# Attention followed by an MLP: equal key chunks, grouped matmuls, and one more unit of lag between the two

## The chip, the cores and the metric

The kernel runs on one core of a Trainium2 chip. The metric is the time of one execution on the device in microseconds (us). Each run also carries a state: on one core, an execution more than 1.5% above the fastest of the same kernel counts as slow and is left out of comparisons. A ratio in this text is the mean time of one kernel's fast runs over that of the other's fast runs of the same rounds, so it is not quite the ratio of the medians quoted beside it. The "granted clock" is the share of PE's full clock that the trace records.

The engines are PE (matmuls; PEld is its weight load), ACT (exponentials, cosines, copies), DVE (vector work), POOL (more vector work) and SP, which here only issues DMAs. Each works through its own list of instructions in the order in which the program emits them and waits for the others by semaphores.

## The reference

```
# q, k, v: [8, 12, 448, 64] f32; tau = 0.1; w_in: [768, 2048]; w_out: [2048, 768]
q_n = q / (norm(q) + 1e-6);  k_n = k / (norm(k) + 1e-6)
attn = softmax(q_n @ k_n.T / tau)          # 448 x 448 for each of 96 heads
x = (attn @ v) laid out as [3584, 768]     # batch and token, head and dim
h = x @ w_in
out = (h * cos(h)) @ w_out                 # [3584, 768] f32
```

## The kernel before

A "unit" is half a batch: six heads, handled as three "pairs" of two heads. There are 16 units and 48 pairs. Two units make one batch of 448 tokens, whose MLP follows later, between the attention work of later units. A batch's first MLP product, with its cosine and its multiplication into gT, is called an MLP block below (8 groups of 12 matmuls); the second product (112 matmuls of 384 columns per batch on average) is doled out in small "fills".

The 448 keys of a head are cut into three chunks of 128 and a tail of 64. In the tail, the two heads of a pair sit in the two halves of the partitions, so its matmuls use other shapes of the PE array:

```python
    def scores(g, c):                       # transposed scores of one chunk, both heads
        j = g % 2
        z = nq[0] % 2                       # two score buffers, SC0 and SC1
        nq[0] += 1
        for a in range(2):
            r = slice(64 * a, 64 * a + 64)
            if c < NC3:                     # chunk of 128 keys
                PE: matmul(sc[:, a, 0:S], qkT[j][r, 128 keys of chunk c], qkT[j][r, 0:S])
            else:                           # tail: 64 keys, output on half of the partitions
                PE: matmul(sc[r, 0, 0:S], qkT[j][r, S : S + TL], qkT[j][r, 0:S])
        ACT: PX[j, c] = exp(sc / TAU)       # 128 x 896, for the tail 128 x 448

    # av_step(g, c): value matmuls of chunk c for both heads, accumulated in bank 0 of AV
    # av_sums(g):    matmuls with ones, 32 columns wide, for the row sums, in bank 1 of AV;
    #                then ACT copies both banks to xu
```
(The bodies are shortened to what is computed.) The row sums go by DMA from xu to another layout ("gather"), DVE takes the reciprocal ("recip"), two more DMAs spread it through DRAM over the partitions ("spread", "broadcast" into RB), and DVE multiplies ("normalise", into xT, the input of the MLP). The order inside a unit, where kq counts steps of one chunk:

```python
    def unit(u, per_quantum):
        for kq in range(4 * UP):
            p, c = kq // 4, kq % 4
            g = UP * u + p
            scores(g, c)
            if c == 1 and g + 1 < NG:
                transposes(g + 1)           # 7 matmuls, then DVE copies to qkT
            # ... loads, squares, norms, scales of unit u + 1 ...
            if u == 0 and kq >= 2 or u == 1:
                load_w(1)                   # one of 10 weight loads
            # ... recip, spread, broadcast, normalise of earlier units ...
            if per_quantum:
                m2_fill(per_quantum[kq % len(per_quantum)])   # 4, 5 or 6 matmuls into PO
            if g >= 1:
                if c in (1, 2):
                    av_step(g - 1, 2 * c - 2)
                    av_step(g - 1, 2 * c - 1)
                if c == 2:
                    av_sums(g - 1)
                if kq == 3:
                    gather(u - 1)
            if u % 2 == 1 and u >= 3 and kq == M1_AT:
                m1((u - 3) // 2)            # the MLP block of the batch before
```

A fill writes one bank, PO, of PSUM, the memory that takes PE's results. After 16 of its matmuls one output half is complete, DVE copies it to osb, and only then can the next half begin.

Of the kernel before, what the change touches and what calls it, by code (L numbers as in the profile page):

```python
# [140 lines left out]
def bass_cosine_attention__then__act_gcu_kernel(  # L141
# [12 lines left out]
    NP2 = NH // 2  # L154
    NU = 2 * B
    UP = 3
    UH = 2 * UP
    NC3 = 3
    MAIN = NC3 * 128
    TL = S - MAIN  # L160
    NS = 7
# [5 lines left out]
    NT = (B * S) // 128  # L167
# [21 lines left out]
    xT = sbs("xT", 2, [128, NP2 * S], BF16)  # L189
    gT = sb("gT", [128, NF * RING], BF16)  # L190
    raw = sbs("raw", 2, [128, UH * NS * D], F32)
    vraw = sb("vraw", [128, UH * 4 * D], F32)
    sq = sbs("sq", UP, [128, 2 * NS * D], BF16)
    n2 = sbs("n2", 2, [128, UH * NS], F32)
    lnn = sbs("lnn", 2, [128, UH * NS], F32)
    rn = sbs("rn", 2, [128, UH * NS], F32)
    qks = sbs("qks", 2, [128, NS * UH * D], BF16)
    va = sbs("va", 2, [128, UH * 4 * D], BF16)
    qkT = sbs("qkT", 2, [128, NS * 128], BF16)
    PX = sbs("PX", 2, [128, 2 * NC3 * S + S], BF16)  # L200
# [4 lines left out]
    ones = sb("ones", [128, 32], BF16)  # L205
    cosb = sbs("cosb", 2, [128, 2 * S], F32)
    osb = sbs("osb", 3, [128, DM], F32)
    ident = sb("ident", [128, 128], BF16)
    iot = sb("iot", [128, 128], I32)
    cst = sb("cst", [128, 4], F32)  # L210
# [5 lines left out]

    W1v = W1.ap().rearrange("p (c n) -> p c n", c=NKC)
    W2v = W2.ap().rearrange("p (f n) -> p f n", f=NF)
    xTv = [t.ap().rearrange("p (c m) -> p c m", c=NP2) for t in xT]
    gTv = gT.ap().rearrange("p (f m) -> p f m", f=NF)  # L220
    rawv = [t.ap().rearrange("p (h s d) -> p h s d", h=UH, s=NS) for t in raw]
    vrawv = vraw.ap().rearrange("p (h c d) -> p h c d", h=UH, c=4)
    qksv = [t.ap().rearrange("p (s h d) -> p s h d", s=NS, h=UH) for t in qks]
    vav = [t.ap().rearrange("p (x c) -> p x c", c=D) for t in va]
    PXm = [t.ap()[:, 0 : 2 * NC3 * S].rearrange("p (c a s) -> p c a s", c=NC3, a=2) for t in PX]
    PXt = [t.ap()[:, 2 * NC3 * S :] for t in PX]
# [5 lines left out]
    PHs = [("SC0", SCv[0]), ("SC1", SCv[1]), ("AV", AVv)]  # L232

    scr = nc.dram_tensor("scr", (NU, UH * S), F32)

    NORM = 11
    M1_AT = 2
# [3 lines left out]
    P.op("POOL", lambda e: e.iota(iot.ap(), [[1, 128]], base=0, channel_multiplier=-1), writes=["iot"])  # L241
# [3 lines left out]
    P.op("POOL", lambda e: e.memset(vrawv[:, :, 3, :], 1.0), writes=["vraw"])  # L245
# [3 lines left out]

    def load(u, p0, p1):  # L250
        i = u % 2
        b, hb = u // 2, UH * (u % 2)
        ha, hn = hb + 2 * p0, 2 * (p1 - p0)
        keys = [("raw", i, p) for p in range(p0, p1)]
        sem = "raw%d_%d" % (i, p0)

        def src(t, tok, n, run):
            return bass.AP(t.tensor, ((b * NH + ha) * S + tok) * D, [[run, n], [S * D, hn], [1, run]])

        h = slice(2 * p0, 2 * p1)  # L260
        P.op("SP", lambda e: e.dma_start(rawv[i][:, h, 0:3, :].rearrange("p h s d -> p h (s d)"),
                                         src(q, 0, 128, NC3 * D)), writes=keys, dma=sem)
        for key_fn in (
            lambda e: e.dma_start(rawv[i][:, h, 4:7, :].rearrange("p h s d -> p h (s d)"),
                                  src(k, 0, 128, NC3 * D)),
            lambda e: e.dma_start(rawv[i][0:TL, h, 3, :], src(q, MAIN, TL, D)),
            lambda e: e.dma_start(rawv[i][64 : 64 + TL, h, 3, :], src(k, MAIN, TL, D)),
        ):
            o = P.op("SP", key_fn, dma=sem)
            for t in keys:  # L270
                P.writer[t] = o

    def load_v(u):
        b, hb = u // 2, UH * (u % 2)

        def src(h0, step, nh, tok, n, run):
            return bass.AP(v.tensor, ((b * NH + hb + h0) * S + tok) * D, [[run, n], [step * S * D, nh], [1, run]])

        P.op("SP", lambda e: e.dma_start(vrawv[:, :, 0:3, :].rearrange("p h c d -> p h (c d)"),
                                         src(0, 1, UH, 0, 128, NC3 * D)), writes=["vraw"], dma="vraw")  # L280
        for a in range(2):
            o = P.op("SP", lambda e, a=a: e.dma_start(vrawv[64 * a : 64 * a + TL, 0::2, 3, :],
                                                      src(a, 2, UP, MAIN, TL, D)), dma="vraw")
            P.writer["vraw"] = o


    def squares(u, p, eng="POOL"):
        i = u % 2
        j = p
        src = raw[i].ap()[:, p * 2 * NS * D : (p + 1) * 2 * NS * D]  # L290
        if eng == "ACT":
            P.op("ACT", lambda e: e.activation(sq[j].ap(), src, ACT.Square), [("raw", i, p)], [("sq", j)])
        else:
            P.op(eng, lambda e: e.tensor_tensor(sq[j].ap(), src, src, ALU.mult), [("raw", i, p)], [("sq", j)])  # L294

    def reduce(u, p):
        i = u % 2
        j = p
        P.op("DVE", lambda e: e.tensor_reduce(out=n2[i].ap()[:, p * 2 * NS : (p + 1) * 2 * NS],  # L299
                                              in_=sq[j].ap().rearrange("p (x d) -> p x d", d=D),  # L300
                                              axis=mybir.AxisListType.X, op=ALU.add),
             [("sq", j)], [("n2", i, p)])

    def rnorm(u, p0, p1):
        i = u % 2
        w = slice(p0 * 2 * NS, p1 * 2 * NS)
        P.op("ACT", lambda e: e.activation(lnn[i].ap()[:, w], n2[i].ap()[:, w], ACT.Ln, bias=cst.ap()[:, 1:2]),
# [4 lines left out]
    def scale(u, p, eng="POOL"):  # L312
        i = u % 2
        h = slice(2 * p, 2 * p + 2)
        P.op(eng, lambda e: e.tensor_tensor(  # L315
            qksv[i][:, :, h, :].rearrange("p s h d -> p h s d"), rawv[i][:, h, :, :],
            bass.AP(rn[i], p * 2 * NS, [[UH * NS, 128], [NS, 2], [1, NS], [0, D]]), ALU.mult),
            [("raw", i, p), ("rn", i, p)], [("qks", i, p)])

    def vcast(u, p):  # L320
        i = u % 2
        P.op("POOL", lambda e: e.tensor_copy(vav[i][:, 8 * p : 8 * p + 8, :],
                                             vrawv[:, 2 * p : 2 * p + 2, :, :].rearrange("p h c d -> p (h c) d")),
             ["vraw"], [("va", i, p)])


    def transposes(g):
        u, p, j = g // UP, g % UP, g % 2
        i = u % 2
        for s in range(NS):  # L330
            P.op("PE", lambda e, s=s: e.transpose(TP.ap()[:, 128 * s : 128 * s + 128],  # L331
                                                  qksv[i][:, s, 2 * p : 2 * p + 2, :], ident.ap()),
                 [("qks", i, p), "ident"], ["TP"])
        P.op("DVE", lambda e: e.tensor_copy(qkT[j].ap(), TP.ap()[:, 0 : NS * 128]), ["TP"], [("qkT", j)])  # L334

    nq = [0]

    def scores(g, c):
        j = g % 2
        z = nq[0] % 2  # L340
        nq[0] += 1
        sc = SCv[z]
        for a in range(2):
            r = slice(64 * a, 64 * a + 64)
            rhs = qkT[j].ap()[r, 0:S]
            if c < NC3:
                P.op("PE", lambda e, r=r, a=a, rhs=rhs: e.matmul(  # L347
                    sc[:, a, 0:S], qkT[j].ap()[r, S + TL + 128 * c : S + TL + 128 * c + 128], rhs,
                    start=True, stop=True), [("qkT", j)], ["SC%d" % z])
            else:  # L350
                P.op("PE", lambda e, r=r, rhs=rhs: e.matmul(  # L351
                    sc[r, 0, 0:S], qkT[j].ap()[r, S : S + TL], rhs, start=True, stop=True),
                    [("qkT", j)], ["SC%d" % z])
        if c < NC3:
            P.op("ACT", lambda e: e.activation(PXm[j][:, c], sc[:, :, 0:S], ACT.Exp, scale=1.0 / TAU),  # L355
                 ["SC%d" % z], [("PX", j, c)])
        else:
            P.op("ACT", lambda e: e.activation(PXt[j], sc[:, 0, 0:S], ACT.Exp, scale=1.0 / TAU),
                 ["SC%d" % z], [("PX", j, c)])

    def av_step(g, c):
        u, p, j = g // UP, g % UP, g % 2
        i = u % 2
        for a in range(2):
            r = slice(64 * a, 64 * a + 64)
            k = slice(0, 128) if c < NC3 else r
            px = PXm[j][:, c, a, :] if c < NC3 else PXt[j][r, :]
            P.op("PE", lambda e, r=r, k=k, a=a, px=px: e.matmul(  # L368
                AVv[r, 0, 0:S], vav[i][k, 8 * p + (4 * a + c if c < NC3 else NC3), :], px, start=(c == 0), stop=(c == NC3)),
                [("va", i, p), ("PX", j, c)], ["AV"])  # L370

    def av_sums(g):
        u, p, j = g // UP, g % UP, g % 2
        i = u % 2
        for c in (0, 1, 2, 3):
            for a in range(2):
                o = slice(64 * a + 32 * (c % 2), 64 * a + 32 * (c % 2) + 32)
                k = slice(0, 128) if c < NC3 else slice(64 * a, 64 * a + 64)
                px = PXm[j][:, c, a, :] if c < NC3 else PXt[j][k, :]
                P.op("PE", lambda e, o=o, k=k, px=px, c=c: e.matmul(  # L380
# [255 lines left out]
```

## Time and profile before

Three runs: 592.94, 594.56 and 594.91 us, median 594.56. A further, profiled run spans 589.0.

The first lines of the page of the kernel before. A busy time is followed by its share of the span and the number of instructions; each digit is the busy share of one fortieth of the span, in tenths:

```profile
span 589.0 us, 7661 instructions
PE 491.1 (83%) x3152; PEld 217.4 (37%) x3152; DVE 234.7 (40%) x300; ACT 290.9 (49%) x358; POOL 192.0 (33%) x159
PE   1380366989998999899898999889898999896997
```

In the first seven fortieths, about 103 us, PE is idle much of the time; after that it is nearly always busy. So there are two regimes: a start-up in which data and its preparation arrive too slowly, and a long stage in which PE sets the pace.

Four of PE's waits in the kernel before (engine, line, tile, who released it: us in total, times, the longest); the left-out ones belong to the start-up or are under 6 us:

```profile
PE SC L347 <- ACT PX L355: 23.6, 3, 21.8
PE PO L477 <- DVE osb L485: 16.0, 22, 2.2
PE SC L351 <- DVE gT L437: 7.1, 3, 2.4
PE AV L432 <- DVE xT L418: 5.2, 1, 5.2
```

The first line is one hole of 21.8 us at 44.7 us. There unit 2's keys come only at 59 us, behind ten weight loads that were all issued during unit 0. The other lines are PE waiting for the copy out of PO, for the last product of an MLP block, and for normalised data.

What PE does inside the long stage is seen in the timeline of one pair before (start, us, line, operation, tile, shape, count). The cost of a group is the distance from its start to the next start, since the shown durations run past the start of the next group:

```profile
120.67 0.38 PE L351 MATMUL SC<-qkT 64*64 64x448 bf16 x2 [2.37 <-DVE gT L437]
120.98 0.82 PE L477 MATMUL PO<-W,gT 128*128 128x384 bf16 x4
121.74 0.36 PE L347 MATMUL SC<-qkT 64*128 64x448 bf16 x2
122.03 0.82 PE L477 MATMUL PO<-W,gT 128*128 128x384 bf16 x4
122.79 0.36 PE L347 MATMUL SC<-qkT 64*128 64x448 bf16 x2
123.08 0.56 PE L331 MATMUL TP<-ident,qks 128*128 128x128 bf16 x7
123.48 0.81 PE L477 MATMUL PO<-W,gT 128*128 128x384 bf16 x4
124.23 0.57 PE L368 MATMUL AV<-PX,va 128*64 128x448 bf16 x4
...
125.78 0.69 PE L368 MATMUL AV<-PX,va 128*64 128x448 bf16 x4
126.39 0.85 PE L380 MATMUL AV<-PX,ones 128*32 128x448 bf16 x8
127.17 0.38 PE L351 MATMUL SC<-qkT 64*64 64x448 bf16 x2
```

The pair takes 127.17 - 120.67 = 6.50 us, although PE never waits inside it. Four PO matmuls take 0.76 us here. In a dense block they take 0.65 (16 of them 2.60). The missing 0.11 us appears wherever the array's shape changes (128\*128 to 64\*128, to 128\*64, to 64\*64), and here the shape changes at nearly every line. (The cut leaves out another score pair and another four PO matmuls.)

### The profile page before, as it was taken

The numbers are of one execution on the slowest core, as the hardware profiler recorded it, in microseconds if no ns is written. First come the engines' busy times: TensorE is split into PE (matmuls) and PEld (weight loads), VectorE is DVE, ScalarE is ACT, GpSimd is POOL, SyncE is SP. The second block draws the span as 40 slices with busy tenths as digits, with TensorE's granted clock in tenths as the row PEclk, the third lists the DMA queues.
The fourth block names the chain that finished last, engine by engine and source line by source line (L and its number), as shares of the span: only waits on it lengthen the run. The fifth ranks groups of instructions, "written<-read, shape, count | busy, mean of one in ns | idle before, by whom it ended". The sixth has DMA issues, their size and how long they took to land.

```text
span 589.0 us, 7661 instructions
## 1 busy us (share of the span) xinstructions
PE 491.1 (83%) x3152; PEld 217.4 (37%) x3152; DVE 234.7 (40%) x300; ACT 290.9 (49%) x358; POOL 192.0 (33%) x159
## 2 busy tenths in 40 slices
PE   1380366989998999899898999889898999896997
PEld 0120122533353444433353444433353344332554
DVE  4300352436444543534345543534354532322421
ACT  3270474466646555556546554555546555550420
POOL 3860854055503480074304380075205240000000
PEclk9996597999999999999999999999999999998999
DMA  6699777015800852045701761145702320122013
GB/s 190 139 225 216 175 191 189 1 50 169 242 3 18 224 143 75 25 115 146 203 2 44 200 170 47 27 123 147 192 1 61 90 76 0 29 77 74 0 55 81
DMA packets 74498, 62.36 MB, mean 106 GB/s; under 512 B 29152, under 2 KB 68064, under 8 KB 74464
## 3 DMA queue, kind: packets, MB, share of 16 engines
q1 hardware_dynamic: 71488, 55.58, 35.4%
q0 software_dynamic: 2976, 6.29, 5.7%
q8 instruction: 25, 0.41, 0.3%
q14 instruction: 9, 0.07, 0.0%
HBM read 56.62 MB, written 11.18 MB: 115 GB/s over the span
## 4 chain that ended last, share of the span: by engine, by line
PE 68%; DMA 15%; DVE 6%; SPq 6%; POOL 2%; ACT 2%; issue 2%; DVEq 0%; ACTq 0%
PE PO L477 20%; PE SC L432 17%; PE AV L432 9%; DMA raw<-in_k_dram 6%; PE AV L368 6%; DMA RB<-scr 5%; PE AV L380 4%; PE SC L347 4%; PE TP L331 3%; PE SC L477 2%; DVE osb L485 2%; DMA sums<-xu 2%; POOL sq L294 2%; PE SC L351 2%; DVE gT L437 1%
## 5 line engine op out<-in xcount | busy, mean ns | idle before, releaser
L355 ACT ACTIVATE PX<-SC 128x896 bf16<-128x896 f32 x144 | 131.2, 918 | 84.8 <-PE SC L347 83.4
L477 PE MATMUL PO<-W,gT 128*128 128x384 bf16 x784 | 155.3, 329 | 19.8 <-DVE osb L485 16.0
L315 POOL TENSOR_TENSOR qks<-raw,rn 128x896 bf16<-128x896 f32 x47 | 79.4, 1689 | 253.5 <-ACT rn L309 253.5
L432 PE MATMUL SC<-xT,W 128*128 128x448 bf16 x516 | 104.4, 359 | 4.2 <-DVE xT L418 4.2
L477 PEld LDWEIGHTS PO<-W,gT 128*128 128x128 bf16 x784 | 65.4, 98 | 76.7 <-DVE osb L485 23.3
L294 POOL TENSOR_TENSOR sq<-raw 128x896 bf16<-128x896 f32 x47 | 80.5, 1739 | 29.3 <-DMA raw<-in_k_dram 29.3
L347 PE MATMUL SC<-qkT 64*128 64x448 bf16 x288 | 53.8, 373 | 34.0 <-ACT PX L355 23.6
L437 DVE TENSOR_TENSOR gT<-SC,cosb 128x896 bf16<-128x896 f32 x43 | 47.0, 1092 | 69.7 <-ACT cosb L435 69.7
L383 ACT ACTIVATE xu<-AV 128x896 f32<-128x896 f32 x48 | 44.0, 917 | 55.9 <-PE AV L380 55.9
L435 ACT ACTIVATE cosb<-SC,cst 128x896 f32<-128x896 f32 x43 | 43.3, 1007 | 56.1 <-PE SC L432 56.1
L432 PEld LDWEIGHTS SC<-xT,W 128*128 128x128 bf16 x516 | 50.9, 99 | 53.8 <-issue 9.2
L299 DVE TENSOR_REDUCE n<-sq 128x14 f32<-128x896 bf16 x48 | 50.7, 1078 | 31.1 <-POOL sq L294 26.9
L368 PE MATMUL AV<-PX,va 128*64 128x448 bf16 (+1 forms) x384 | 61.9, 380 | 0.0
L432 PE MATMUL AV<-xT,W 128*128 128x448 bf16 x252 | 53.4, 364 | 7.2 <-DVE xT L418 5.2
L418 DVE TENSOR_TENSOR xT<-xu,RB 128x448 bf16<-128x448 f32 x48 | 38.2, 808 | 51.3 <-DMA RB<-scr 51.3
L334 DVE COPY qkT<-TP 128x896 bf16<-128x896 bf16 x48 | 29.8, 621 | 65.3 <-PE TP L331 65.3
L485 DVE COPY osb<-PO 128x384 f32<-128x384 f32 x49 | 27.1, 554 | 57.3 <-PE PO L477 57.3
L331 PE MATMUL TP<-ident,qks 128*128 128x128 bf16 x336 | 28.8, 230 | 21.0 <-POOL qks L315 11.0
L347 PEld LDWEIGHTS SC<-qkT 64*128 64x128 bf16 x288 | 13.8, 93 | 81.1 <-issue 36.6
L435 ACT ACTIVATE cosb<-AV,cst 128x896 f32<-128x896 f32 x21 | 21.1, 1007 | 42.7 <-PE AV L432 42.7
L380 PE MATMUL AV<-PX,ones 128*32 128x448 bf16 (+1 forms) x384 | 40.9, 361 | 0.0
L437 DVE TENSOR_TENSOR gT<-AV,cosb 128x896 bf16<-128x896 f32 x21 | 22.9, 1092 | 38.1 <-ACT cosb L435 38.1
(35 smaller groups left out, 246.8 us busy)
## 6 DMA issues: line engine op xcount, KB each, us to landing
RB<-scr SPq DMA_DIRECT2D x32, 336.0 KB, 4.6
vraw<-in_v_dram SPq DMA_DIRECT2D x16, 576.0 KB, 4.6
raw<-in_q_dram SPq DMA_DIRECT2D x15, 576.0 KB, 5.9
raw<-in_k_dram SPq DMA_DIRECT2D x15, 576.0 KB, 6.4
out_dram<-osb SPq DMA_DIRECT2D x32, 192.0 KB, 2.7
out_dram<-osb SPq DMA_DIRECT2D x12, 384.0 KB, 2.9
W<-in_moe_w_in_dram POOLq DMA_DIRECT2D x6, 512.0 KB, 10.7
W<-in_moe_w_out_dram POOLq DMA_DIRECT2D x4, 768.0 KB, 20.1
```

The costliest lines, as they stand in the source:

```text
L294: P.op(eng, lambda e: e.tensor_tensor(sq[j].ap(), src, src, ALU.mult), [("raw", i, p)], [("sq", j)])
L299: P.op("DVE", lambda e: e.tensor_reduce(out=n2[i].ap()[:, p * 2 * NS : (p + 1) * 2 * NS], in_=sq[j].ap().rearrange("p (x d) -> p x d", d=D ...
L315: P.op(eng, lambda e: e.tensor_tensor(qksv[i][:, :, h, :].rearrange("p s h d -> p h s d"), rawv[i][:, h, :, :], bass.AP(rn[i], p * 2 * NS, ...
L331: P.op("PE", lambda e, s=s: e.transpose(TP.ap()[:, 128 * s : 128 * s + 128], qksv[i][:, s, 2 * p : 2 * p + 2, :], ident.ap()), [("qks", i, ...
L347: P.op("PE", lambda e, r=r, a=a, rhs=rhs: e.matmul(sc[:, a, 0:S], qkT[j].ap()[r, S + TL + 128 * c : S + TL + 128 * c + 128], rhs, start=Tr ...
L355: P.op("ACT", lambda e: e.activation(PXm[j][:, c], sc[:, :, 0:S], ACT.Exp, scale=1.0 / TAU), ["SC%d" % z], [("PX", j, c)])
L368: P.op("PE", lambda e, r=r, k=k, a=a, px=px: e.matmul(AVv[r, 0, 0:S], vav[i][k, 8 * p + (4 * a + c if c < NC3 else NC3), :], px, start=(c ...
L380: P.op("PE", lambda e, o=o, k=k, px=px, c=c: e.matmul(AVv[o, 1, 0:S], ones.ap()[k, :], px, start=(c < 2), stop=(c >= 2)), ["ones", ("PX", ...
L432: P.op("PE", lambda e, n=n, c=c, a=a: e.matmul(ph[:, a, 0:S], W1v[:, c, 128 * n : 128 * n + 128], xTv[b % 2][:, c, :], start=(c == 0), sto ...
L435: P.op("ACT", lambda e: e.activation(cosv[cz], ph[:, :, 0:S], ACT.Sin, bias=cst.ap()[:, 0:1], scale=1.0), [name, "cst"], [("cos", cz)])
L437: P.op("DVE", lambda e: e.tensor_tensor(gTv[:, 2 * gidx : 2 * gidx + 2, S * (b % 2) : S * (b % 2) + S], ph[:, :, 0:S], cosv[cz], ALU.mult) ...
L477: P.op("PE", lambda e, po=po, f=f, col=col, hf=hf: e.matmul(po[:, 0:HW], gTv[:, f, col : col + 128], W2v[:, f, HW * hf : HW * hf + HW], st ...
```

## The change

It has five parts:

1. The keys are cut into four chunks of 112 with no tail, so all chunks have one shape and every load is a run of 1 KB. The tail's exponential grows from 448 to 896 columns, and the squares and scales on POOL from 896 to 1024 elements.
2. Two chunks of scores are issued together, and all AV matmuls and sums of a pair in one block.
3. Fills come in blocks of 8 instead of 4 to 6, and 16 stand behind each MLP block, to cover the wait for gT.
4. An MLP block comes one unit later, so that its input has long been normalised. Until the MLP starts, DVE instead of ACT copies AV to xu.
5. Weights come in 20 pieces, six per unit, instead of 10 nearly at once.

The diff cut to its core (cuts marked with "..."):

```diff
-    NC3 = 3
-    MAIN = NC3 * 128
-    TL = S - MAIN
-    NS = 7
+    NJ = 4
+    NP = S // NJ
+    NS = 2 * NJ
...
     def scores(g, c):
-        j = g % 2
-        z = nq[0] % 2
+        j, z = g % 2, c % 2
...
+            P.op("PE", lambda e, r=r, a=a: e.matmul(
+                SCv[z][0:NP, a, 0:S], qkT[j].ap()[r, S + NP * c : S + NP * c + NP], qkT[j].ap()[r, 0:S],
+                start=True, stop=True), [("qkT", j)], ["SC%d" % z])
+        P.op("ACT", ... ACT.Exp ...)          # one form for every chunk
...
+    LAG = 4
+    FILLS = ((8, 8, 8, 8, 8, 8, 8, 8, 8, 0, 8, 0), (8, 8, 8, 8, 16, 8, 8, 8, 8, 8, 8, 16))
...
+    def around(u, kq):                        # all work off PE, by step, as in unit() before
+        ...
+        if kq % 2 == 1:
+            load_w()
+        if u >= 1:
+            if kq == 2:
+                gather(u - 1)
+            if kq == 5:
+                recip(u - 1)
+                spread(u - 1)
+            if kq == 8:
+                broadcast(u - 1)
+        if u >= 2 and kq < UP:
+            normalise(u - 2, kq)
...
     for u in range(NU):
-        b = (u - 3) // 2
-        ...
-        unit(u, fills)
+        for p in range(UP):
+            g = UP * u + p
+            scores(g, 0)
+            scores(g, 1)
+            if g >= 1:
+                attend(g - 1, "DVE" if u < LAG else "ACT")
+            around(u, 4 * p)
+            m2_fill(steps.pop(0) if steps else 0)
+            if g + 1 < NG:
+                transposes(g + 1)
+            around(u, 4 * p + 1)
+            scores(g, 2)
+            scores(g, 3)
+            around(u, 4 * p + 2)
+            m2_fill(steps.pop(0) if steps else 0)
+            around(u, 4 * p + 3)
+            if p == 0 and u >= LAG and u % 2 == 0:
+                m1((u - LAG) // 2)            # 8 groups, then m2_fill(16)
+                steps = list(FILLS[((u - LAG) // 2) % 2])
...
+    # tail: the last but one MLP block, m2_fill(16), m2_fill(80), the last block, m2_fill(16), the rest
```

## The prediction

> **What bounds the kernel now.** The page: PE busy 83% of a 589.0 us span. By windows: to 97.8 us is start-up, PE busy 40 us; then six periods of about 65 us (two units, one MLP block), PE 58 to 62 us busy at full clock; from 525 an MLP tail. Start-up is bound by loads and POOL, the rest by PE. PE's list of waits: 21.8 us at 44.7 (timeline: unit 2's k lands only at 59, behind ten weight loads issued in unit 0; DMA share 1.14 there), 16.0 us on the osb copy of the one PO bank, 7.1 us after MLP blocks on gT, 9.4 us on xT.
>
> **PE costs, start to start in the timeline.** A pair (120.67 to 127.17) takes 6.50 us with 16 second-MLP matmuls. Dense ones take 0.1625 us, so 3.9 us is attention. Every change of array shape costs 0.10 to 0.12 us: 4 second-MLP matmuls 0.76 instead of 0.65, one score pair 0.29 instead of 0.19, four AV 0.50 instead of 0.375. The Trainium skill (TensorEngine Tiling (Array Packing), Key Properties) says that changing the tiling mode drains the TensorE; these starts agree. Four scores in a row took 0.49: the drain is per group.
>
> **The change on PE.** Per pair: two groups of four scores 0.98, AV in one group 0.88, sums as two concurrent fours 0.50 (0.78 before: the tail made extra shapes), transposes 0.41, two second-MLP groups of 8, 2.82. Sum 5.6 us against 6.5. I add 0.3 because the second score buffer's exponential (0.92 us) ends just when the next score step wants it. Period: 6 x 5.9 + first MLP 18.2 + 16 matmuls behind it 2.6 = 56; with 1.5 of stalls 57.5, against 65.4. The 16 matmuls cover the gT wait and the table load; groups of 8 put the osb copy under attention work. Six periods: about -47 us.
>
> **Costs added.** ACT: the tail's exponential goes from 539 to 918 ns, 4.6 us per pair, below PE's 5.9. POOL squares and scales grow by 8/7, to 13.3 us per unit. One more unit passes without MLP; a batch of MLP moves into the tail.
>
> **Start-up.** Weights go out six pieces per unit, so unit 2's k no longer waits. POOL with issues takes about 17 us per unit; about 18.6 MB must land, at up to 240 GB/s (the saturated window). Loads become 1 KB runs (768 and 256 B before); the skill (DMA: Bandwidth & Descriptors, Specifications) wants at least 512 B for line rate; the page counts 29152 packets under that. I expect the first MLP block at 88 to 95 us (97.8 before), one unit further on.
>
> **Tail.** Two first-MLP blocks 36.4, about 240 second-MLP matmuls 39, stalls 4, end 4.3: about 85 us, without the 5.2 us wait on xT.
>
> **Sum.** 92 + 338 + 85 = 515 span; timed runs lie 5.5 above it: 520. With 2 for stalls unseen: 522 us, range 503 to 548. Chances: faster 0.96, within 2% 0.03, slower 0.01.
>
> **Right or wrong.** Distance of MLP blocks in the PE timeline 57 us (wrong if over 61); a plain pair 5.6 to 6.0 us; sums group 0.5 us; no 22 us gap near 45 us; PE waits on osb under 8 us; PE share above 86%.
>
> **What would make it wrong.** POOL or loads keeping start-up at 100 us or more; ACT (exponentials and the AV copy in one queue) ruling the pairs; DVE, in order, held up by RB and delaying qkT; 112-wide matmuls that do not overlap as 128-wide ones do.

## The result, and the profile after

The kernel after takes 541.41 us (median of 4 runs, 538.33 to 543.38), against 594.73 for the kernel before in the same rounds. The ratio is 0.910, with a 95% interval of 0.905 to 0.915. All four runs are fast ones, and the profiled one spans 538.9 us.

The page of the kernel after:

```profile
span 538.9 us, 7716 instructions
PE 471.6 (88%) x3200; PEld 230.7 (43%) x3200; DVE 257.7 (48%) x311; ACT 288.4 (54%) x344; POOL 220.5 (41%) x169
PE   1477674798999999999999999999899999779896
```

The long stage is denser now: almost only nines. The start-up is not shorter. Eight fortieths of this shorter span, 108 us, stay below nine.

One pair of the kernel after, from the timeline. PE waits for nothing in it that the view marks:

```profile
193.14 0.69 PE L314 MATMUL SC<-qkT 64*112 64x448 bf16 x4
193.76 0.95 PE L325 MATMUL AV<-PX,va 112*64 112x448 bf16 x8
194.64 0.56 PE L331 MATMUL AV<-PX,ones 112*32 112x448 bf16 x8
195.13 1.47 PE L420 MATMUL PO<-W,gT 128*128 128x384 bf16 x8
196.44 0.56 PE L305 MATMUL TP<-ident,qks 112*128 112x112 bf16 x8
196.93 0.59 PE L314 MATMUL SC<-qkT 64*112 64x448 bf16 x4
197.45 1.47 PE L420 MATMUL PO<-W,gT 128*128 128x384 bf16 x8
```

Seven groups instead of twelve, the same 16 PO matmuls, and 5.71 us (the next pair starts at 198.85) instead of 6.50. The lines also show that a new group alone costs nothing: the eight PO matmuls at 195.13 take 1.31 us to the transposes, which use the full array as they do (dense ones take 1.30), and those at 197.45 take 1.40 to the scores, whose shape differs.

Three of PE's waits in the kernel after (two left out, of 10.8 and 8.1 us, belong to the start-up, and the other three are 2.4 us or less):

```profile
PE SC L314 <- ACT PX L317: 16.7, 26, 2.4
PE SC L314 <- DVE qkT L308: 13.6, 5, 5.2
PE PO L420 <- DVE osb L428: 9.5, 12, 3.1
```

The hole of 21.8 us is gone, as are the waits on xT. Another has grown: scores waiting for qkT, 13.6 us in five pieces, all before 110 us (3.3 us in the kernel before). Of the first line, 11.8 us fall into the same stretch.

The span can be split at two events in the timeline: the start of the first MLP block, and the start of the first of the two blocks that run after the last attention.

| | predicted | kernel after |
|---|---|---|
| first MLP block starts | 92 us | 110.1 us |
| from there to the first tail block | 338 us | 334.5 us |
| from there to the end | 85 us | 94.3 us |
| span | 515 us | 538.9 us |

In the kernel before, the first MLP block starts at 97.8 us, with one unit less done, and the six periods to the seventh block take 390.4 us. So the periods went from 65.1 to 55.75 us, a gain of 56 us, while the start-up was 18 us and the tail 9 us longer than I had said.

**Where the start-up went.** The timeline of DVE in the kernel after (the bracket gives its idle time and what ended it):

```profile
64.00 2.06 DVE L371 TENSOR_TENSOR xT<-xu,RB 128x448 bf16<-128x448 f32 x1 [1.59 <-DMA RB<-scr]
65.98 0.61 DVE L308 COPY qkT<-TP 128x896 bf16<-128x896 bf16 x1
```

PE had finished the transposes behind that qkT copy at 62.05. The copy started only at 65.98, because the normalising stands before it in DVE's list: it waited 1.59 us for the DMA that fills RB and then took 2.06 us itself (0.61 the next time). PE's next scores waited with it, 3.69 us. PE was slow here besides: eight AV matmuls took 1.71 us at 58.69, against 0.95 in the pair above. The Trainium skill (Perfetto Trace Analysis, Tensor Engine Instruction) calls ACT, DVE and GPSIMD "strict FIFO", and here the trace shows it for DVE.

SP's list in the same stretch shows what these DMAs meet:

```profile
56.57 1.10 SPq L364 DMA_DIRECT2D RB<-scr  x2
58.17 0.32 SPq L259 DMA_DIRECT2D vraw<-in_v_dram  x1
58.53 0.57 SPq L252 DMA_DIRECT2D raw<-in_q_dram  x1
59.15 1.98 SPq L252 DMA_DIRECT2D raw<-in_k_dram  x1
62.44 5.99 SPq L345 DMA_DIRECT2D sums<-xu  x1
```

The DMAs that fill RB were issued before the loads, so no queue held them up; the second landed at 63.98, 6.9 us later, while the loads moved beside it. The gather of the next sums is another matter. It is four DMAs of 5 KB, each normally issued in 0.6 us. Here it comes behind 2 MB of loads for a later unit, and the first takes 6 us to issue. Up to 110 us, sums take 9.2 us (median) from issue to landing, against 3.8 us in the same stretch of the kernel before. The two figures are not quite like for like: in the kernel before, the loads hold SP before the gather is issued (one for 14.04 us, at 28.83), and that time is not in them. In e_schedule below, the median is 3.6 us and the start-up no shorter.

DVE's waits up to 110 us in the kernel after that concern this round trip, and POOL's main wait from 12 to 110 us:

```profile
DVE rcp L353 <- DMA sums<-xu: 14.0, 3, 6.3
DVE xT L371 <- DMA RB<-scr: 6.1, 2, 4.5
POOL qks L290 <- ACT rn L283: 21.9, 4, 9.9
```

POOL, which I had expected to set the pace, waits 22 us for norms. Those come from DVE's sums of squares, which stand in the same list.

**Where the tail went.** The timeline behind the first tail block:

```profile
462.74 1.46 PE L420 MATMUL PO<-W,gT 128*128 128x384 bf16 x8
464.04 1.09 DVE L386 TENSOR_TENSOR gT<-SC,cosb 128x896 bf16<-128x896 f32 x1 [1.18 <-ACT cosb L384]
465.05 1.69 DVE L371 TENSOR_TENSOR xT<-xu,RB 128x448 bf16<-128x448 f32 x3
466.65 0.55 DVE L428 COPY osb<-PO 128x384 f32<-128x384 f32 x1
467.26 4.26 PE L420 MATMUL PO<-W,gT 128*128 128x384 bf16 x16 [3.06 <-DVE osb L428]
```

The same 16 matmuls take 2.77 us elsewhere. After the wait of 3.06 us they took 4.26, on a slower clock (PE's granted clock is 0.93 from 462.7 to 487.4). Five more waits of about 0.7 us follow, one per half, because there is only one PO bank. The tail also held 264 second-MLP matmuls instead of my 240. Two entries of the fill list, 8 and 16, are never used before the loop ends.

### The profile page after: what moved, and what is told of

Same layout as the page of the kernel before. It is cut to its first block, busy times and chain, and to the rows that moved or that the text cites. A ratio compares the mean times of both kernels' runs of the same rounds, so it can differ in the third digit from the quotient of the medians.

```text
span 538.9 us, 7716 instructions
## 1 busy us (share of the span) xinstructions
PE 471.6 (88%) x3200; PEld 230.7 (43%) x3200; DVE 257.7 (48%) x311; ACT 288.4 (54%) x344; POOL 220.5 (41%) x169
## 2 busy tenths in 40 slices
DMA packets 51490, 62.36 MB, mean 116 GB/s; under 512 B 9984, under 2 KB 44288, under 8 KB 51456
## 4 chain that ended last, share of the span: by engine, by line
PE 64%; DMA 16%; DVE 10%; ACT 4%; SPq 3%; POOL 2%; issue 1%; DVEq 0%; ACTq 0%
PE PO L420 20%; PE SC L381 16%; PE AV L381 10%; DMA sums<-xu 6%; DMA RB<-scr 6%; PE AV L325 5%; PE SC L314 5%; PE AV L331 3%; DMA raw<-in_k_dram 3%; DVE xT L371 3%; ACT PX L317 3%; PE SC L420 2%; DVE n L273 2%; PE TP L305 2%; SPq L345 2%; DMA scr<-rcp 2%
## 5 line engine op out<-in xcount | busy, mean ns | idle before, releaser
L317 ACT ACTIVATE PX<-SC 112x896 bf16<-112x896 f32 x192 | 164.0, 915 | 85.8 <-PE SC L314 85.8
L290 POOL TENSOR_TENSOR qks<-raw,rn 112x1024 bf16<-112x1024 f32 (+1 forms) x48 | 90.5, 1884 | 193.1 <-ACT rn L283 193.0
L314 PE MATMUL SC<-qkT 64*112 64x448 bf16 x384 | 70.4, 428 | 32.6 <-ACT PX L317 16.7
L269 POOL TENSOR_TENSOR sq<-raw 112x1024 bf16<-112x1024 f32 x47 | 92.2, 1985 | 9.0 <-DMA raw<-in_k_dram 8.9
L273 DVE TENSOR_REDUCE n<-sq 112x16 f32<-112x1024 bf16 x48 | 57.5, 1209 | 7.7 <-ACT sq L267 4.1
L325 PE MATMUL AV<-PX,va 112*64 112x448 bf16 x384 | 54.5, 414 | 0.0
L314 PEld LDWEIGHTS SC<-qkT 64*112 64x112 bf16 x384 | 21.8, 136 | 66.8 <-ACT PX L317 34.7
L305 PE MATMUL TP<-ident,qks 112*128 112x112 bf16 x384 | 31.8, 235 | 18.8 <-POOL qks L290 10.8
L381 PEld LDWEIGHTS AV<-xT,W 128*128 128x128 bf16 x288 | 27.7, 98 | 29.4 <-issue 2.9
L305 PEld LDWEIGHTS TP<-ident,qks 112*128 112x128 bf16 x384 | 26.1, 109 | 32.7 <-POOL qks L290 14.7
```

What stands on the lines that cost most here:

```text
L269: P.op(eng, lambda e: e.tensor_tensor(sq[p].ap(), x, x, ALU.mult), [("raw", i, p)], [("sq", p)])
L273: P.op("DVE", lambda e: e.tensor_reduce(out=n2[i].ap()[:, p * 2 * NS : (p + 1) * 2 * NS], in_=sq[p].ap().rearrange("p (x d) -> p x d", d=D ...
L290: P.op(eng, lambda e, s0=s0, s1=s1: e.tensor_tensor(qksv[i][:, s0:s1, h, :].rearrange("p s h d -> p h s d"), rawv[i][:, h, s0:s1, :], bass ...
L305: P.op("PE", lambda e, s=s: e.transpose(TP.ap()[:, NP * s : NP * s + NP], qksv[i][:, s, 2 * p : 2 * p + 2, :], ident.ap()), [("qks", i, p, ...
L314: P.op("PE", lambda e, r=r, a=a: e.matmul(SCv[z][0:NP, a, 0:S], qkT[j].ap()[r, S + NP * c : S + NP * c + NP], qkT[j].ap()[r, 0:S], start=T ...
L317: P.op("ACT", lambda e: e.activation(PXv[j][:, c], SCv[z][0:NP, :, 0:S], ACT.Exp, scale=1.0 / TAU), ["SC%d" % z], [("PX", j, c)])
```

## The experiments

My theory for the start-up (theory 1) was the round trip sums, reciprocal, RB: its small DMAs stand behind bulk loads, and DVE waits for them in order. Its rivals were POOL's work (theory 2) and the bytes themselves (2b). For the long stage the questions were how much comes from the order of the matmuls, how much from the layout, and what the lag is worth. Twelve kernels ran, in four jobs, each beside the kernel before (594 to 596 us in each).

| run | fast runs, median us | ratio to before | first MLP block | six periods | to the end |
|---|---|---|---|---|---|
| after | 541.4 | 0.910 | 110.1 | 334.5 | 94.3 |
| a_ring | 534.7 | 0.901 | 105.1 | 333.4 | 94.4 |
| b_squares | 542.4 | 0.913 | 112.3 | 335.5 | 94.2 |
| c_lag3 | 550.0 | 0.925 | 92.2 | 360.8 | 94.1 |
| e_schedule | 550.7 | 0.926 | 110.1 | 342.6 | 94.4 |
| f_pacing | 588.7 | 0.989 | 89.7 | 394.9 | 101.7 |
| g_split | 561.0 | 0.944 | 105.9 | 356.5 | 94.2 |
| i_slack | 528.4 | 0.889 | 99.9 | 330.1 | 94.1 |
| d2_tail | 554.3 | 0.932 | 109.8 | 333.3 | 107.1 |
| l_slack_tail | 553.1 | 0.928 | 107.6 | 332.7 | 112.0 |
| k_best | 544.9 | 0.915 | 100.7 | 332.8 | 107.3 |
| n_ring_tail | 531.0 | 0.893 | 105.2 | 333.2 | 91.2 |

The last three columns come from the PE timeline of the one profiled run of each. "Six periods" is from the first MLP block to the seventh. In the kernel before, f_pacing and c_lag3, that stretch begins one unit earlier. In g_split and i_slack two of four runs, and in k_best two of six, counted as slow and are left out; their granted clocks (0.946 to 0.958) are not lower than those of many fast runs, so what made them slow is not known.

The kernel after ran in another job than its variants, and single traces scatter: d_tail, d2_tail and g_split have the start-up of the kernel after unchanged, and their first block starts at 111.9, 109.8 and 105.9 us. A difference of less than some 6 us in that column shows nothing unless it comes again or stands beside such a run of the same job.

### a_ring: the bulk loads from another queue

```diff
-            o = P.op("SP", lambda e, x=x, t=t: e.dma_start(          # q and k
+            o = P.op("ACT" if u >= 2 else "SP", lambda e, x=x, t=t: e.dma_start(
...                                                                    # v likewise
-        if kq == 9 and u + 2 < NU:
+        if kq == 11 and u + 2 < NU:
             load_v(u + 2)
```

> The kernel after, with the bulk loads of q, k and v (from unit 2 on) issued from the ACT queue instead of the SP queue, v two steps later; the same bytes, at nearly the same time. Theory 1 (start-up is bound by the round trip sums, reciprocal, RB, whose small DMAs stand behind 2 MB of loads in the same queue, and by DVE waiting in order for them): sums land in 3 to 4 us in the first 110 us instead of 9.2, the first MLP block starts at 92 to 99 us instead of 110.1, time 525 to 533. Theory 2 (start-up is bound by POOL's work or by the bytes): first MLP block within 2 us of 110, time 541.

Correct, 534.7 us, with the first MLP block at 105.1. Sums landed in 7.1 us instead of 9.2, and DVE's wait for them fell from 14.0 to 2.1 us. Its wait for RB did not fall (7.1 us). The result lies between the two theories. The time is about 7 us less than that of the kernel after, and 8 less than that of b_squares in the same job, so the queue (or v's later load, which came with it) is a part; most of the 18 us is not explained by it. The block alone would not show it, given the scatter, but n_ring_tail below has it at 105.2 again. The Trainium skill (DMA: Bandwidth & Descriptors, Issuing engines are not separate DMA queues) says that issuing from several engines only saves the time on the sequencer, "which is usually small relative to the DMA itself". The landing times agree in part, since the loads still share the DMA engines with the sums. The issue time that was saved was not small here, though: 6 us for a DMA of 5 KB.

### b_squares: less work for POOL

```diff
-                squares(u + 1, kq)
+                squares(u + 1, kq, "ACT" if 1 <= u <= 3 and kq else "POOL")
```

> The kernel after, with two of three squares per unit moved from POOL to ACT while units 1 to 3 run: 3.8 us less work for POOL per unit. Theory 1 (DMA round trip and DVE in order): first MLP block within 3 us of 110.1, time 538 to 544. Theory 2 (POOL's work bounds start-up): first MLP block at 99 to 103, time 531 to 535.

Correct, 542.4 us, with the first MLP block at 112.3. POOL only waits longer for the norms (30.9 us instead of 21.9). Theory 2 is out: POOL's work did not bound the start-up.

### c_lag3: the old lag

```diff
-    LAG = 4
+    LAG = 3
...
-            if p == 0 and u >= LAG and u % 2 == 0:
+            if p == 0 and u >= LAG and u % 2 == 1:
...   # tail: one block fewer; recip, spread and broadcast of the last unit between fills of 16
```

> The kernel after, with the MLP lagging by three units as before, all else kept. If the added unit of lag pays for itself by taking the RB wait out of the way: slower, 543 to 548. If start-up is starved of PE work anyway: the first MLP block starts at 93 to 97 with one unit of attention fewer done, the tail has one MLP block fewer, and the time is 531 to 539. I lean to the second.

Correct, 550.0 us: slower, and I had leaned to the other side. The first block does start early, at 92.2 us, but the blocks now wait for their input. PE's longest entry in the wait list of c_lag3:

```profile
PE AV L381 <- DVE xT L371: 20.0, 7, 4.1
```

Seven of the eight blocks wait, 0.7 to 4.1 us each. After four of these waits the first 12 matmuls of the block also run slowly (3.7 to 4.6 us instead of 2.43). In this order the extra unit of lag is worth 8.6 us, net of the start-up that it lengthens. It is not the price of a lag of three as such: the kernel before has that lag too, and only its first and last blocks wait for xT (4.2 and 5.2 us). The kernel after normalises one step later in the unit than the kernel before; a lag of three with the earlier step was not run in the new order.

### d_tail: fills between the groups of the last block, first attempt

```diff
-    m2_fill(16 * 5)
     for gi in range(NF // 2):
         m1_group(B - 1, gi)
+        m2_fill(10)
```

> The kernel after, with the five halves of second-MLP work in the tail spread between the groups of the last first-MLP block, so that the copy out of the one PO bank hides. If the tail's 9 us over my estimate are the copies of the single bank (five boundaries at 0.83 us over 2.60, and one of 3.06 with a slow clock behind it): from the start of the first tail block to the end 86 to 88 us instead of 94.3, time 533 to 536. If they come from elsewhere: no change.

The result was wrong (relative error 0.096), and the kernel took 552.7 us. The fault was mine: 40 matmuls of batch 5 are still queued when the loop ends, not 16, and 24 of them were now emitted after the last block had begun to overwrite their input in gT. They also waited for each product. The run says nothing about the tail.

### e_schedule: the order without the layout

The kernel before, with chunks of 128 and a tail, but with the loop, fills, lag, weight pieces and tail of the kernel after:

```diff
+    def attend(g, eng):
+        for c in range(4):
+            av_step(g, c)
+        av_sums(g, eng)
...   # the unit loop, load_w, m1 and the tail taken from the kernel after
```

> The other half of the change: the kernel before with its chunks of 128 and tail of 64, but the order, weight pieces, lag and fills of the kernel after. Per pair three shape changes more (tail scores, tail AV, tail sums) and 0.19 us for the tail's sums, so about 0.5 us more than after: a plain pair 6.2, time 553 to 562. If the layout carries most of the gain: 570 or more; if it carries none: 541.

Correct, 550.7 us, 2 us below the range. The order, with the lag, the fills and the pacing, carries most of the gain: 45 us of it (595.6 to 550.7) come without any change of layout, and the layout adds about 9 (to 541.4, in another job). From one pair of e_schedule in the timeline, its AV and sums:

```profile
194.57 1.06 PE L368 MATMUL AV<-PX,va 128*64 128x448 bf16 x8
195.56 0.85 PE L380 MATMUL AV<-PX,ones 128*32 128x448 bf16 x8
196.34 1.48 PE L482 MATMUL PO<-W,gT 128*128 128x384 bf16 x8
```

The pair takes 6.06 us (194.09 to 200.15), 0.35 more than after: 0.29 in the sums (195.56 to 196.34, against 0.49), 0.11 in AV, and 0.06 back in the scores. (In that pair of the kernel after, the second half of the first score group started only when an exponential had freed its buffer, so its 0.62 us contains about 0.1 of waiting.) The start-up is the same in both, 110.1 us. The kernel after has far fewer short packets (9984 under 512 B in the whole run, instead of 29312 in e_schedule), so those do not seem to have set the pace of the start-up; the layouts differ in more than this. The skill (DMA: Bandwidth & Descriptors, Specifications) asks for at least 512 B for line rate; no run here shows a gain from it in this place.

### f_pacing: the weight pieces alone

```diff
-            if u == 0 and kq >= 2 or u == 1:
-                load_w(1)
+            if kq % 2 == 1:
+                load_w()
```
(with the 20 pieces of the kernel after)

> The kernel before with only the weight loads changed: 20 pieces, one at every second step, as in after. The 21.8 us gap near 45 us goes; the first MLP block starts at 80 to 90 us instead of 97.8; periods stay at 65 us; time 578 to 588. If start-up is held by the sums and RB round trip as after is, the block starts no earlier than 95 and the time stays above 590.

Correct, 588.7 us, ratio 0.989 (0.981 to 0.998). The hole of 21.8 us is gone, but the first block comes only 8 us earlier, at 89.7. In place of the hole, DVE waits 17.5 us for sums and 18.8 us for RB in the first 112 us (7.1 and 12.9 in the kernel before). By the test set beforehand this speaks against the round trip as what holds this kernel's start-up (block no earlier than 95, time above 590); the block came at the late end of the other range, and the time just above it. The trace leaves open how much is the round trip and how much the load of the DMA engines, whose share is 0.98 from 45 us to the block.

### g_split: four more changes of shape per pair

```diff
+            n = steps.pop(0) if steps else 0
             scores(g, 0)
+            m2_fill(n // 2)
             scores(g, 1)
...
-            m2_fill(steps.pop(0) if steps else 0)
+            m2_fill(n - n // 2)
...   # the same for chunks 2 and 3
```

> The kernel after, with each score group cut in two by half of the second-MLP matmuls that follow it, so that a pair has four more changes of array shape and the same matmuls. If a change of shape costs 0.11 us as read from the starts: 0.44 us more in about 36 pairs, a plain pair 6.15 instead of 5.71, time 553 to 560. If what counted was the removal of tails and waits: within 3 us of 541.

Correct, 561.0 us. A pair in the timeline takes 6.80 us (255.02 to 261.82), of which 0.63 is a wait for the osb copy. Without the wait it is 6.17, and 6.15 was expected, so the price of 0.11 us per change holds (0.46 us for four). The total is a little above the range because the shorter fills also bring back the osb wait: 8.2 us from 166 to 405 us, where the kernel after has 1.3 us from 166 to 391.

### i_slack: a third AV buffer, so that DVE waits later

```diff
-    xu = sbs("xu", 2, [128, 2 * UP * S], F32)
+    xu = sb("xu", [128, 5 * UP * S], F32)     # three AV parts, two sums parts
...
-            if kq == 5:
+            if kq == 9:
                 recip(u - 1)
                 spread(u - 1)
-            if kq == 8:
+            if kq == 11:
                 broadcast(u - 1)
-        if u >= 2 and kq < UP:
-            normalise(u - 2, kq)
+        if u >= 2 and 6 <= kq < 9:
+            normalise(u - 2, kq - 6)
```

> The kernel after, with a third buffer for the unnormalised AV result, so that the reciprocal can stand four steps later in DVE's order, the broadcast three and the normalising six: seven steps instead of three between a DMA's issue and DVE's wait for it. The same work and bytes; the loads keep their queue. Theory 1 (DVE waits in order for sums and RB and so holds up qkT and the sums of squares): DVE's waits for these DMAs in the first 110 us fall from 26 us to under 6, the first MLP block starts at 90 to 100 instead of 110.1, time 525 to 534. Theory 2b (the bytes bound start-up: DMA share 0.84 to 0.90 there): block at 106 or later, and POOL waits for raw instead; time 538 to 542.

(The 26 us that I name there as DVE's waits in the kernel after were misread; they are 20.1.) Correct, fast runs 525.9 and 530.8 us, and two runs counted as slow at 535.3 and 537.7, at the same granted clock (0.956 to 0.958), so 528.4 may flatter it; the median of all four is 533.1. The first block starts at 99.9, against 105.9 in g_split of the same job. DVE's waits up to 99.9 us in the profiled run:

```profile
DVE xT L376 <- DMA RB<-scr: 8.3, 2, 4.8
DVE rcp L358 <- DMA sums<-xu: 5.0, 3, 1.8
```

These are 13.3 us instead of 20.1, not under 6. POOL's wait for norms falls from 21.9 to 8.8 us. From 45 us to the first block the DMA share is now 0.98 at 209 GB/s, against 0.88 at 181 GB/s in the kernel after. So a third of the waits went, and the DMA engines came close to being always busy. The sum of DVE's waits does not by itself set the start-up, though: in g_split they are 25.8 us, more than in the kernel after, and its block comes 4 us sooner.

### d2_tail, l_slack_tail, k_best: the tail, second attempt, alone and combined

```diff
     for gi in range(NF // 2):
         m1_group(b, gi)
+        m2_fill(5)
...
-    m2_fill(16)
     m2_add(b)
-    m2_fill(16 * 5)
     for gi in range(NF // 2):
         m1_group(B - 1, gi)
+        m2_fill(10)
```

> The mended tail test. The first one gave a wrong result: 40 matmuls of batch 5, not 16, are still queued when the loop ends, and 24 of them came after the last first-MLP block had begun to overwrite their input. Now the 40 go between the groups of the first tail block (5 each), and 80 of batch 6 between those of the last (10 each), 16 behind it. If the tail's extra 9 us are the copies of the one PO bank: from the start of the first tail block to the end 85 to 88 us instead of 94.3, time 532 to 536. If not: 541.

> The third AV buffer with its later waits, and the mended tail. The two act at different ends, so their gains should add: 8 and 7 us off 541, time 522 to 530, first MLP block at 100, tail 86 to 88.

> The same, with the bulk loads from the ACT queue as well. In the slack run the DMA share was 0.96 to 1.00 from 45 to 100 us, so the bytes bound start-up there: then a second queue adds nothing and the first MLP block stays at 98 to 102, time within 3 us of the run without it. If the queue still costs: block at 94 to 97, 517 to 524.

All three are correct and all have a longer tail: 107.1, 112.0 and 107.3 us instead of 94.3. The timeline of d2_tail shows part of why:

```profile
448.47 0.65 PE L420 MATMUL PO<-W,gT 128*128 128x384 bf16 x3
449.71 1.09 DVE L386 TENSOR_TENSOR gT<-SC,cosb 128x896 bf16<-128x896 f32 x1 [1.99 <-ACT cosb L384]
450.72 0.55 DVE L428 COPY osb<-PO 128x384 f32<-128x384 f32 x1
451.33 0.50 PE L420 MATMUL PO<-W,gT 128*128 128x384 bf16 x2 [2.20 <-DVE osb L428]
```

A half ends in the middle of a fill. Its copy stands behind the gT product of the group just issued, which waits for a cosine, so PE stands for 2.2 us instead of 0.7. It is DVE's order again, this time by my own hand. Of the 12.8 us that the tail grew, 5.7 are waits on osb (13.7 instead of 8.0) and 3.6 a wait of the last block for xT. The granted clock in the tail was 0.95 instead of 0.98, which by my estimate (0.05 x 107 - 0.02 x 94) makes up the rest.

The gain of i_slack did not come back in l_slack_tail. Its first block starts at 107.6 us, with DVE waiting 20.8 us for the round trip, and its time (553.1) is level with d2_tail's (554.3, block at 109.8) in the same job. With the loads on the ACT queue as well (k_best), the block starts at 100.7 and the fast runs are 8 us better. In k_best the chain is nearly gone: DVE no longer waits for sums and waits 6.3 us for RB, POOL waits 3.5 us for norms instead of 21.9, and PE's scores wait 6.6 us for DVE instead of 13.6. POOL now waits 9.5 us for the loads (2.6 in the kernel after from 12 us on), and from 45 us to the block the DMA share is 1.03 at 216 GB/s. So of the 18 us, the chain was worth about 9 in this job, and behind it the loads themselves seem to hold the start-up at about 100 us.

### n_ring_tail: fills that end with a half

```diff
     for gi in range(NF // 2):
         m1_group(b, gi)
+        m2_fill(8)
...
-    m2_fill(16)
     m2_add(b)
-    m2_fill(16 * 5)
     for gi in range(NF // 2):
         m1_group(B - 1, gi)
+        if gi < 5:
+            m2_fill(16)
```
(and the loads on the ACT queue, as in a_ring)

> The bulk loads on the ACT queue as in the first queue run, and the tail mended once more. In the second tail run the copies were emitted behind the gT product of the group just issued, and DVE, in order, came to them only 2 us after the group's end: waits of PE on osb in the tail were 13.7 us there. Now every half of 16 ends with its block of fills: 8, 8, 8, 8, 8 between the first tail groups and 16 behind each of five of the last. If that order was the cause: PE waits on osb in the tail under 4 us, from the start of the first tail block to the end 86 to 88 us (94.3 in after, 107 in the second tail run), time 525 to 530. If the interleaving itself costs (array, clock, PSUM): tail stays above 94, time 535 or more.

Correct, 531.0 us (six fast runs, 529.4 to 533.9), ratio 0.893 (0.889 to 0.896). This is the steadiest of the versions that beat both kernels. PE's waits in its tail, from 438 us on:

```profile
PE AV L381 <- DVE xT L371: 4.0, 1, 4.0
...
PE PO L420 <- DVE osb L428: 0.7, 1, 0.7
```

The waits on osb fell from 13.7 us in d2_tail (8.0 in the kernel after) to 0.7, so the order on DVE was their cause. The tail shrank only to 91.2 us, not to 86 to 88, because the last block now comes sooner than its normalised input. It waits 4.0 us for xT, and its first 12 matmuls take 4.64 us instead of 2.43.

## Why the prediction was right or wrong

The time, 541.4 us, lies inside the range, 19 us above the middle. The direction and the main mechanism were right, and two terms of the sum were mis-sized.

- **Cost of a change of shape: right.** A plain pair takes 5.71 us (5.6 to 6.0 said), the sums group 0.49 (0.50 said). Doing the opposite (g_split) added 0.46 us for four changes once the osb wait is taken off. The Trainium skill (TensorEngine Tiling (Array Packing), Key Properties) names the drain but gives no size; this case gives 0.11 us.
- **Periods of about 57.5 us: right, a little too high.** They are 55.75 us. With the 24 matmuls that moved to the tail they would be about 0.65 us longer. The 0.3 us per pair that I added for the second score buffer was mostly not there: from 166 to 391 us PE waits 3.2 us in all for exponentials.
- **The parts of the gain.** Order with lag, fills and pacing: 45 us. Layout: 9. Pacing alone: 7, about 1%. The lag is worth 8.6 us in this order (c_lag3). I had not separated these, and in c_lag3 I leaned the wrong way. Within the six periods (56 us), 36 pairs that are 0.79 us shorter make 28 us by estimate, PE's waits fell from some 26 us to some 10, and the moved matmuls are 4: the shapes are about half of it.
- **"I expect the first MLP block at 88 to 95 us": wrong**, 110.1. I reckoned the start-up as the larger of POOL's work and the bytes. What filled the gap was a chain: a small DMA behind bulk loads, DVE waiting for it in order, and qkT and the norms behind DVE. I had listed "DVE, in order, held up by RB and delaying qkT" among what could go wrong, but gave it no time. b_squares rules out POOL. a_ring and i_slack each show a part of the chain, and in k_best, where it is nearly gone, the block comes 9 us sooner than in d2_tail of the same job. The other 9 us are the bytes, as far as k_best tells: I had put 18.6 MB at up to 240 GB/s, which by estimate is 78 us, and the kernel after moved about 20 MB at 183 GB/s before its first block, k_best the same at 201.
- **"Tail ... about 85 us": too low**, 94.3. Some 4 us are the 24 matmuls that I did not count (at 0.1625 us each), and the rest is the single PO bank: 8.0 us of waits, where I had 4 for all stalls, and the slow clock behind the longest.
- **"Timed runs lie 5.5 above" the span: wrong**, and it happened to hide 4 us of the error. I had set the median of the timed runs against the span of another execution. One and the same run lies 1.8 us above its span, before (590.76 and 589.0) and after (540.68 and 538.9).
- **Waits on osb under 8 us: wrong**, 9.5, of which 8.0 are in the tail. In the long stage they have nearly gone, as said. PE share above 86%: right, 88%.

What stays open: how the remaining start-up is shared between the order on DVE and the DMA engines' load. k_best speaks for about half each, but it is one job. i_slack gained 13 us against the kernel after of another job, and l_slack_tail only 1 us against d2_tail of its own, and the waits in their traces differ accordingly. No run changed the number of bytes.

## What to carry to other kernels

Where matmuls of different array shapes alternate, count the changes of shape: at 0.11 us each they can cost more than a stall that catches the eye. Here the order gave 45 us, with its fills, lag and pacing, and making the shapes uniform 9. Before predicting a stage that is not bound by PE, follow the in-order list of every engine that waits for a DMA and ask what stands behind that wait; neither the busy time of an engine nor a sum of bytes shows it. When work is put between other work to hide a copy, place it so that the copy is not emitted behind something that waits longer.

## What the Trainium skill lacked or had wrong

- TensorEngine Tiling (Array Packing), Key Properties: the drain at a change of tiling mode has no figure. Here it is 0.10 to 0.12 us per change, read from starts (4 matmuls of 384 columns 0.76 us instead of 0.65), and confirmed by adding four changes per pair (5.71 to 6.17 us).
- DMA: Bandwidth & Descriptors, Issuing engines are not separate DMA queues: the saving on the sequencer is called usually small. Here the issue of a 5 KB DMA took 6.0 us on the queue that had just issued 2 MB of loads (0.6 us as a rule), and moving the loads to another issuing engine, with v two steps later, gained about 7 us of 541 between two jobs.
- DMA: Bandwidth & Descriptors, Specifications: going from 29312 to 9984 packets under 512 B changed nothing that these runs could see in the start-up (first MLP block at 110.1 us in e_schedule and in the kernel after). The two layouts differ otherwise too, so this does not contradict the page.
- TensorE: Matmul & The Clock Gate, Part 1: the clock is said to fall back after an idle window of about 3.4 us. Its table under "Why this matters for your kernels" speaks of gaps over about 3 us. Here less was enough: a wait of PE of 3.06 us (16 matmuls behind it took 4.26 us instead of 2.77), and in the kernel after one of 2.38 us at 131.91 (eight AV matmuls took 1.71 instead of 0.95). The same wait of 2.37 us in i_slack, at 120.61, left the clock at full. One of 3.98 us in n_ring_tail made 12 matmuls take 4.64 us instead of 2.43. The waits of 3 to 4 us cost 1.5 to 2.2 us more behind them.
